# Scatters of the tokens' places that no longer name one another as a dependency

## The chip, the cores and the metric

The kernel runs on one core of a Trainium2 chip. The metric is device time in microseconds of one execution. Five instruction queues work side by side: TensorE (PE: matrix products and transposes), VectorE (DVE), ScalarE (ACT), GpSimd (POOL) and SyncE (SP, which issues DMAs). An engine takes its own instructions strictly in order; between engines, and between an engine and a DMA, order comes from semaphores alone.

## What is computed

Three layers follow one another; the numbers below are the reference's, cut to what matters.

```
attention:  4 x 8 heads, 576 positions, head_dim 64, causal by blocks of 64
            -> x of shape [2304 tokens, 512]
MLP:        h = x @ w_in (512 x 2048); g = max(h,0) + alpha*min(h,0); x = g @ w_out
experts:    logits = x @ w_gate (512 x 8); expert = argmax(logits); gate = softmax(logits)[expert]
            for e in 0..7:  out[tokens of e] = gate * (max(x @ w1[e], 0) @ w2[e])
```

Each token goes to exactly one expert, so before the expert stage the kernel must know, for each expert, which tokens it has and with which gate weight.

## The kernel before, in words

The 2304 tokens are worked in nine groups of 256 (`G`), two tiles of 128 tokens each (`GT` = 2). Attention of later batches, the first MLP and the routing of finished groups are interleaved in one plan: each piece of work is a task with the engines that may do it, an estimated duration, a priority and the buffers that it reads and writes. The planner (`Plan.order`) simulates the tasks and writes them out in the order of its simulated starts. The program is built with a manual schedule, so the order on each engine is that of this plan; the framework adds the semaphores that the data need.

For a group of the first MLP, TensorE makes 16 blocks `l` (line 697), VectorE applies the activation (`t`, lines 675 and 676), ScalarE or VectorE makes the high part `gh` (line 700), POOL or VectorE the low part `gl` (line 703), and TensorE adds `gh` and `gl` times `wo` into `acc` (line 727). In the attention, POOL or VectorE scales the probabilities `P` (line 530) before TensorE transposes them into `PT` (line 519).

The routing of a group (class `Route`) makes logits, the expert of each token, and the token's place in that expert's list. The list is a table in DRAM, `info`, of 8 x 2304 rows with two columns of four bytes: the token's number and its gate weight. `place` computes the places `si` and fills `ig`, both columns for both tiles: column 0 (the token's number) by one POOL add over both tiles (line 853), column 1 by VectorE (line 858). Then `scatter` (line 861) writes one tile's 128 rows of `ig` into `info` at the places `si`, by an indirect DMA of POOL; there are two scatters for each group, eighteen in all. `ig` and `si` have one buffer each.

At the start, the DMA of line 1343 fills the whole of `info` with a sentinel. The readers of `info` are loads on SP: `fetch_it` (line 1418) loads the first 256 rows of the expert that leads after eight groups, while the ninth group is still in the first MLP; `fetch` (line 1000, and 1002 for the remainder) loads the next 256 rows each time. With the loaded list `it`, POOL gathers rows of `x2` into `xg` (lines 1424 and 1004), and TensorE transposes them into `Tx` (line 1011).

For the group's gate logits the buffer `xr` is shared by two things: the tokens of the next group (line 646) and rows of the gate's weights (line 768), which VectorE multiplies with the tokens (line 813). `xr` has one buffer. From the tokens, ScalarE and VectorE make `xh` and `xl` (lines 654 and 657), the inputs of line 697.

Of the kernel before, what the change touches and what calls it, by code (L numbers as in the profile page):

```python
# [12 lines left out]
ALU = mybir.AluOpType  # L13
# [3 lines left out]
IOA = bass.IndirectOffsetOnAxis  # L17
ENGINES = [getattr(mybir.EngineType, e) for e in ("PE", "DVE", "Activation", "Pool", "SP")]

P = 128  # L20
# [7 lines left out]
G = P * GT  # L28
# [18 lines left out]
class Consts:  # L47
    def __init__(K, nc, cp):
        K.ident = cp.tile([P, P], F32, name="ident")
        make_identity(nc, K.ident)  # L50

        K.U = cp.tile([P, P], F32, name="U")
        nc.gpsimd.memset(K.U, 1.0)
        nc.gpsimd.affine_select(K.U, K.U, pattern=[[1, P]], compare_op=ALU.is_gt, fill=0.0, base=0, channel_multiplier=-1)

        K.II = cp.tile([P, 64], F32, name="II")
        nc.vector.tensor_add(K.II, K.ident[:, 0:64], K.ident[:, 64:128])
        K.ones = cp.tile([P, P], F32, name="ones")
        nc.gpsimd.memset(K.ones, 1.0)
        K.w8 = cp.tile([P, E], F32, name="w8")  # L60
        nc.gpsimd.iota(K.w8, pattern=[[-1, E]], base=E, channel_multiplier=0, allow_small_or_imprecise_dtypes=True)
        K.i8 = cp.tile([1, E], F32, name="i8")
        nc.gpsimd.iota(K.i8, pattern=[[1, E]], base=0, channel_multiplier=0, allow_small_or_imprecise_dtypes=True)
        K.base = cp.tile([1, E], F32, name="base")
        nc.gpsimd.iota(K.base, pattern=[[NT, E]], base=0, channel_multiplier=0, allow_small_or_imprecise_dtypes=True)

        K.run = [cp.tile([P, GT + 1, E], F32, name=f"run{i}") for i in range(2)]
        nc.gpsimd.iota(K.run[0][:, 0], pattern=[[NT, E]], base=0, channel_multiplier=0, allow_small_or_imprecise_dtypes=True)
        K.pid = cp.tile([P, GT], I32, name="pid")
        nc.gpsimd.iota(K.pid, pattern=[[P, GT]], base=0, channel_multiplier=1)  # L70
        K.zero = cp.tile([P, DM // P], F32, name="zero")
        nc.vector.memset(K.zero, 0.0)
        K.wg = cp.tile([P, 4, E], F32, name="wg")
        K.al = cp.tile([P, 16], F32, name="al")
# [154 lines left out]
class Weights1:  # L229
# [13 lines left out]
    def plan(A, pl):  # L243

        nc = A.nc
        for i, (key, src) in enumerate(A.srcs):
            s, pr, r = ("stw", i), WPRIO + WSTEP * i, A.raw[key]
            x, y = (r.rearrange("p (n t) -> p n t", t=2)[:, :, z] for z in range(2))
            pl.buf(s, "stw", (P, 512), I32)

            def load(on, r=r, src=src):
                nc.sync.dma_start(r, src.bitcast(I32))

            def scale(on, y=y):
                nc.scalar.mul(y.bitcast(F32), y.bitcast(F32), 2.0 ** -112)

            def sign(on, y=y, s=s):
                nc.gpsimd.tensor_tensor(pl[s].bitcast(F32), y.bitcast(F32), A.K.zero[:, 0:1].to_broadcast([P, 512]), op=ALU.mult)

            def bits(on, x=x, y=y, s=s, key=key):  # L260
                nc.vector.scalar_tensor_tensor(pl[s], x, 29, pl[s], op0=ALU.logical_shift_right, op1=ALU.bitwise_or)
                nc.vector.scalar_tensor_tensor(A.raw[key][:, 0:512], y, 3, pl[s], op0=ALU.logical_shift_left, op1=ALU.bitwise_or)

            pl.add(("SP", 450), load, [], [("r", key)], 100 * i, (524288, 360))
            pl.add(("ACT", 700), scale, [], [("r", key)], pr)
            pl.add(("POOL", 1100), sign, [("r", key)], [s], pr)
            pl.add(("DVE", 1450), bits, [("r", key)], [s, ("w", key)], pr)
# [343 lines left out]
class Mlp1:  # L611


    def __init__(A, tc, K, W1, bp, rt, psp, xT, wgT, x2, info):
        A.tc, A.nc, A.K, A.W1, A.W, A.bp, A.rt, A.psp, A.wgT = tc, tc.nc, K, W1, W1.W, bp, rt, psp, wgT
        A.xT, A.x2, A.info = xT, x2, info

    def plan(A, pl):
        for g in range(NG):
# [167 lines left out]
class Route:  # L787
# [5 lines left out]
    def small(A, nm, shape, dt=F32):  # L793
        return A.ml.rt.tile([P] + shape, dt, tag="r" + nm, bufs=1, name=nm + A.n)
# [45 lines left out]
    def place(A, rk):  # L840
        nc, K, g, GE, oh, ex, sm, small = A.nc, A.K, A.g, GT * E, A.oh, A.ex, A.sm, A.small
        run = K.run[g % 2]
        for i in range(GT):
            nc.vector.tensor_add(run[:, i + 1], run[:, i], rk[:, E * i:E * i + E])
        nc.vector.tensor_copy(K.run[(g + 1) % 2][:, 0], run[:, GT])
        pos, sl, A.si = small("pos", [GT, E]), small("sl", [GT]), small("si", [GT], I32)
        nc.vector.tensor_add(pos, run[:, 0:GT], rk[:, GE:2 * GE].rearrange("p (i e) -> p i e", e=E))
        nc.vector.tensor_mul(pos, pos, oh)
        nc.vector.reduce_sum(sl, pos, axis=AX.X)
        nc.vector.tensor_copy(A.si, sl)  # L850

        A.ig, gx, ge = small("ig", [GT, 2], I32), small("gx", [GT, E]), small("ge", [GT])
        nc.gpsimd.tensor_scalar(A.ig[:, :, 0], K.pid, g * G, None, op0=ALU.add)
        nc.vector.tensor_scalar_add(sm, sm, 1e-9)
        nc.vector.tensor_mul(gx, ex, oh)
        nc.vector.reciprocal(sm, sm)
        nc.vector.reduce_sum(ge, gx, axis=AX.X)
        nc.vector.tensor_mul(A.ig[:, :, 1].bitcast(F32), ge, sm)

    def scatter(A, i):  # L860
        A.nc.gpsimd.indirect_dma_start(out=A.ml.info, out_offset=IOA(ap=A.si[:, i:i + 1], axis=0), in_=A.ig[:, i, :], in_offset=None)

    def steps(A, psp, xts):

# [72 lines left out]
class Experts:  # L937
# [59 lines left out]
    def fetch(A, r, j, base, rows=NT + 1):  # L997
        it = A.itile(r, j)
        src = A.info[ds(base + 2 * P * j, 2 * P), :].rearrange("(h p) c -> p h c", p=P)
        A.nc.sync.dma_start(it, src)  # L1000
        if j:
            A.nc.sync.dma_start(A.rem, src)
        for h in range(2):
            A.nc.gpsimd.indirect_dma_start(out=A.xg[:, h], out_offset=None, in_=A.x2[0:rows, :], in_offset=IOA(ap=it[:, h, 0:1], axis=0))
# [296 lines left out]
def moe_kernel(tc, qk, v, qke, ve, w_in, w_out, alpha, w_gate, wgT, w1, w2, out):  # L1301
    nc = tc.nc
    with ExitStack() as ctx:
# [3 lines left out]
        info = dp.tile([E * NT, 2], I32, name="info")  # L1307
# [3 lines left out]
        K = Consts(nc, cp)  # L1311
# [4 lines left out]
        ap = st0.enter_context(tc.tile_pool(name="attn", bufs=1))  # L1316
        aps = st0.enter_context(tc.tile_pool(name="attnps", bufs=1, space=PSUM))
        pl, banks, hold = Plan(), Slots(), {}
# [10 lines left out]
        ml = Mlp1(tc, K, W1, bp, cp, None, xT, wgT, x2, info)  # L1329
        od = Order(nc, K, cp)  # L1330

        def setup():

            pl.buf(("sent",), "xt", (P, E * NT // P, 2), I32)
            pl.buf(("alr",), "t", (16, P))
            pl.buf(("alps",), "T")

            def sentinel(on):
                nc.gpsimd.memset(pl["sent",], 0)
                nc.gpsimd.memset(pl["sent",][:, :, 0:1], NT)  # L1340

            def empty(on):
                nc.sync.dma_start(info.rearrange("(p n) c -> p n c", p=P), pl["sent",])
                nc.sync.dma_start(x2[NT:NT + 1, :].rearrange("o (p n) -> p (o n)", p=P), K.zero)

            def load(on):
                nc.sync.dma_start(K.wg, w_gate.rearrange("(k p) e -> p k e", p=P))
                nc.sync.dma_start(pl["alr",], alpha.rearrange("(f p) -> f p", p=P))

            pl.add(("POOL", 600), sentinel, [], [("sent",)], 1000)  # L1350
            pl.add(("SP", 900), empty, [("sent",)], [("info0",)], 1000, (160000, 100))
            pl.add(("SP", 900), load, [], [("wg",), ("alr",)], -4000, (20000, 10))
            pl.add(("PE", 120), lambda on: nc.tensor.transpose(pl["alps",][:, 0:16], pl["alr",], K.ident[0:16, 0:16]), [("alr",)], [("alps",)], -250)
            pl.add(("DVE", 160), lambda on: nc.vector.tensor_copy(K.al, pl["alps",][:, 0:16]), [("alps",)], [("al",)], -250)

        def close(on):
            st0.close()
            psc = ctx.enter_context(tc.tile_pool(name="ps", bufs=1, space=PSUM))
            banks.add(psc, T=1, H=3)
            banks.add(psb, T=2, H=2)  # L1360
            ccp = ctx.enter_context(tc.tile_pool(name="experts", bufs=1))
            ex = hold["ex"] = Experts(tc, K, wp, ccp, banks, x2, info, w1, w2, out)
            ex.rawtiles(ccp, NR)

        def first_expert(done):
# [49 lines left out]

        def fetch_it():
            ex = hold["ex"]
            nc.sync.dma_start(ex.itile(0, 0), info[ds(hold["base"], 2 * P), :].rearrange("(h p) c -> p h c", p=P))

        def fetch_rows():  # L1420
            ex = hold["ex"]
# [11 lines left out]
        ex = hold["ex"]  # L1433
# [60 lines left out]
```

## Time and profile before

| | |
|---|---|
| median of 3 runs | 955.63 us |
| the three runs | 955.39, 955.63, 960.72 us |
| profiled execution, its own time | 954.17 us |
| its span, first to last instruction | 952.4 us |
| TensorE busy | 880.6 us (92%) |
| VectorE, ScalarE, POOL busy | 560.2, 402.2, 310.6 us |
| mean granted TensorE clock | 0.973 |

Starts in the profile are counted from the start of the span. A number in brackets at the end of a timeline row is the idle time of that engine just before the row, with what ended it by the profile; where a wait names several semaphores, the profile puts it down to the one that came last by its records, which need not be the right one. The granted clock is given in parts of 2.4 GHz: 1.00 is 2.4 GHz, 0.50 is 1.2 GHz.

### The profile page before, as it was taken

How to read it: one execution, taken by the hardware profiler on the slowest of the kernel's cores; microseconds unless marked ns; L12 is line 12 of the kernel's file. 1: busy time of each engine (PE TensorE's matmuls, PEld its weight loads, DVE VectorE, ACT ScalarE, POOL GpSimd, SP SyncE). 2: the span in 40 equal slices, each digit the busy share in tenths (PEclk: the TensorE clock that was granted, in tenths of full speed). 3: DMA queues.
4: the chain of work that ended last, by engine and by line, in shares of the span. 5: the costliest groups of instructions: out<-in, count | busy, mean ns of one | idle time of the engine just before them, and what ended most of it. 6: DMA issues, size and time to landing. Idle time of an engine off the chain costs nothing. (4 is left out here: it accounts for less than half of the span.)

```text
span 952.4 us, 17816 instructions
## 1 busy us (share of the span) xinstructions
PE 880.6 (92%) x6185; PEld 750.1 (79%) x6185; DVE 560.2 (59%) x1387; ACT 402.2 (42%) x1022; POOL 310.6 (33%) x323
## 2 busy tenths in 40 slices
PE   7999989999989999989999989899889998998883
PEld 6656658888878888878899889889779987988763
DVE  5999896667757767847756656446215211513450
ACT  7877764455435554445421111223215222523451
POOL 1455665333433354443332222232212111111110
PEclk9999999999999999999999989999999999999997
DMA  9981001313213214302112212033436211613551
GB/s 344 372 311 51 18 17 52 99 47 115 97 50 106 85 50 139 100 22 73 58 49 70 48 64 67 24 113 109 142 115 219 71 47 56 211 48 92 157 182 42
DMA packets 49724, 98.39 MB, mean 103 GB/s; under 512 B 12575, under 2 KB 19375, under 8 KB 49584
## 3 DMA queue, kind: packets, MB, share of 16 engines
q1 hardware_dynamic: 38720, 76.78, 24.6%
q0 software_dynamic: 4240, 11.56, 3.9%
q10 hardware_dynamic: 6624, 8.39, 2.5%
q8 instruction: 63, 1.03, 0.5%
q14 instruction: 77, 0.63, 0.2%
HBM read 83.43 MB, written 13.67 MB: 102 GB/s over the span
## 5 line engine op out<-in xcount | busy, mean ns | idle before, releaser
L697 PE MATMUL l<-xh,wi 128*128 128x256 f32 x1024 | 208.6, 288 | 1.7 <-DVE t L676 1.7
L697 PEld LDWEIGHTS l<-xh,wi 128*128 128x128 f32 x1024 | 169.5, 193 | 6.6 <-DVE t L676 2.2
L727 PE MATMUL acc<-wo,gh 128*128 128x512 f32 x512 | 168.4, 410 | 0.0
L697 PE MATMUL l<-xl,wi 128*128 128x256 f32 x512 | 146.0, 285 | 0.0
L703 POOL TENSOR_TENSOR gl<-t,gh 128x256 fp32r<-128x256 f32 x107 | 81.5, 762 | 183.3 <-ACT gh L700 150.7
L700 ACT CAST gh<-t 128x256 fp32r<-128x256 f32 x120 | 48.8, 406 | 178.4 <-DVE t L676 105.8
L675 DVE TENSOR_SCALAR t<-l,al 128x256 f32<-128x256 f32 x128 | 61.8, 483 | 104.2 <-PE l L697 98.3
L530 POOL TENSOR_SCALAR P<-P,sm 128x256 f32<-128x256 f32 (+4 forms) x71 | 89.0, 1260 | 101.9 <-ACT gh L700 46.2
L727 PE MATMUL acc<-wo,gl 128*128 128x512 f32 x256 | 102.1, 399 | 8.9 <-POOL gl L703 8.9
L697 PEld LDWEIGHTS l<-xl,wi 128*128 128x128 f32 x512 | 99.1, 194 | 3.9 <-issue 0.2
L727 PEld LDWEIGHTS acc<-wo,gh 128*128 128x128 f32 x512 | 88.0, 193 | 10.9 <-issue 0.5
L524 ACT COPY F<-PT 128x384 f32<-128x384 f32 (+2 forms) x126 | 58.5, 479 | 70.5 <-PE PT L519 68.6
L479 DVE TENSOR_REDUCE nb<-S 128x1 f32<-128x256 f32 (+4 forms) x160 | 69.5, 476 | 28.4 <-PE S L456 14.8
L813 DVE SCALAR_TENSOR_TENSOR xt<-y,xr_wg 128x512 f32<-128x512 f32 x96 | 73.7, 768 | 8.9 <-DMA xr_wg<-in_wgT_dram 5.1
L519 PE MATMUL PT<-ident,P 128*128 128x128 f32 (+1 forms) x400 | 65.7, 284 | 12.2 <-POOL P L530 6.7
L496 ACT ACTIVATE P<-S,nb 128x128 f32<-128x128 f32 (+3 forms) x128 | 66.7, 529 | 9.3 <-DVE nb L479 8.4
L519 PEld LDWEIGHTS PT<-ident,P 128*128 128x128 f32 (+1 forms) x400 | 45.9, 142 | 26.5 <-POOL P L530 9.4
L727 PEld LDWEIGHTS acc<-wo,gl 128*128 128x128 f32 x256 | 48.9, 191 | 21.2 <-POOL gl L703 10.2
L1038 PE MATMUL l<-cxh,e 128*128 128x256 f32 x320 | 58.2, 282 | 0.8 <-ACTq L1273 0.8
L1038 PE MATMUL Y<-e,hh 128*128 128x512 f32 x176 | 57.2, 406 | 0.0
L676 DVE SCALAR_TENSOR_TENSOR t<-l,t 128x256 f32<-128x256 f32 x128 | 54.3, 425 | 4.4
L995 DVE TENSOR_TENSOR e<-raw,e 128x512 fp32r<-128x512 f32 x68 | 43.9, 685 | 19.6 <-ACT e L994 19.4
(375 smaller groups left out, 1686.5 us busy)
## 6 DMA issues: line engine op xcount, KB each, us to landing
raw<-in_moe_w_dram SPq DMA_DIRECT2D x96, 256.0 KB
xr_wg<-in_wgT_dram SPq DMA_DIRECT2D x24, 512.0 KB
qk<-in_qk_dram SPq DMA_DIRECT2D x16, 608.0 KB
rawi<-in_moe_w_in_dram SPq DMA_DIRECT2D x16, 512.0 KB
rawo<-in_moe_w_out_dram SPq DMA_DIRECT2D x16, 512.0 KB
v<-in_v_dram SPq DMA_DIRECT2D x16, 320.0 KB
x<-y ACTq DMA_DIRECT2D x16, 256.0 KB
xr<-xT SPq DMA_DIRECT2D x7, 512.0 KB
```

Of the source, the lines that this page charges most:

```text
L479: nc.vector.tensor_reduce(pl["nb", p, c][:, 2 * k + j:2 * k + j + 1], pl[Ss[j]][:, a:b], axis=AX.X, op=ALU.max, negate=True)
L496: nc.scalar.activation(pl[x][:, a:b], pl[Ss[j]][:, a:b], AF.Exp, bias=nb, scale=1.0, accum_out=pl["sm", p, c][:, 2 * k + j:2 * k + j + 1])
L519: nc.tensor.transpose(pl[t][0:w, k], pl[x][:, P * k:P * k + w], A.K.ident)
L524: f(pl[F][:, 0:n], pl[t][:, 0:n])
L530: (nc.gpsimd if on == "POOL" else nc.vector).tensor_scalar(y, y, pl["sm", p, c][:, k:k + 1], None, op0=ALU.mult)
L675: nc.vector.tensor_scalar(pl[out], x, 0.0, A.K.al[:, f:f + 1], op0=ALU.min, op1=ALU.mult)
L676: nc.vector.scalar_tensor_tensor(pl[out], x, 0.0, pl[out], op0=ALU.max, op1=ALU.add)
L697: nc.tensor.matmul(pl[l][:, 0:G], lhsT=a[:, c], rhs=b, start=k == 0 and j == 0, stop=k == 3 and j == 2)
L703: (nc.gpsimd if on == "POOL" else nc.vector).tensor_sub(pl[gl], pl[t], pl[gh].bitcast(F32))
L727: nc.tensor.matmul(pl[acc], lhsT=x[:, c], rhs=w, start=f == 0 and j == 0, stop=f == 15 and j == 2)
L813: A.nc.vector.scalar_tensor_tensor(t, A.y(i), 1.0, wg, op0=ALU.mult, op1=ALU.mult, accum_out=A.L()[:, i, e:e + 1])
L1038: A.nc.tensor.matmul(ps, lhsT=x[a], rhs=w[b], start=first and q == 0, stop=last and q == 2)
```

## The change

The tokens' numbers (column 0 of `ig`) are now made for one tile at a time, by a new method `token`, just ahead of that tile's scatter. A scatter is put into a group of instructions, `places`, whose members have no dependency on one another through `info`. What they would have had through it is named by hand: each scatter follows the sentinel's fill (`filled`); the first load of the list (`fetch_it`) follows all scatters made until then, and the load of the first expert's second tile follows the scatters made since.

```diff
@@ class Mlp1
+        A.sent, A.filled = [], None
+
+    def follow(A, x, ys):
+        for y in ys:
+            A.tc.add_manual_dep(x.ins, y.ins.name, mybir.DependencyInfo(mybir.DependencyClass.Sync, mybir.DependencyReason.DATA), reason="places")
+
+    def placed(A, x):
+
+        A.follow(x, A.sent)
+        A.sent = []
@@ Route.place
-        nc.gpsimd.tensor_scalar(A.ig[:, :, 0], K.pid, g * G, None, op0=ALU.add)
@@ Route
+    def token(A, i):
+        A.nc.gpsimd.tensor_scalar(A.ig[:, i, 0:1], A.K.pid[:, i:i + 1], A.g * G, None, op0=ALU.add)
+
     def scatter(A, i):
-        A.nc.gpsimd.indirect_dma_start(out=A.ml.info, out_offset=IOA(ap=A.si[:, i:i + 1], axis=0), in_=A.ig[:, i, :], in_offset=None)
+
+
+        A.token(i)
+        ml = A.ml
+        x = A.nc.gpsimd.indirect_dma_start(out=ml.info, out_offset=IOA(ap=A.si[:, i:i + 1], axis=0), in_=A.ig[:, i, :], in_offset=None)
+        ml.tc.declare_no_dep(x.ins, group="places", reason="rows of their own")
+        ml.tc.add_to_no_dep_group("places", x.ins)
+        ml.follow(x, [ml.filled])
+        ml.sent.append(x)
@@ Experts.fetch
-        A.nc.sync.dma_start(it, src)
+        x = A.nc.sync.dma_start(it, src)
+        if (r, j) == (0, 1):
+            A.ml.placed(x)
@@ moe_kernel
-                nc.sync.dma_start(info.rearrange("(p n) c -> p n c", p=P), pl["sent",])
+                ml.filled = nc.sync.dma_start(info.rearrange("(p n) c -> p n c", p=P), pl["sent",])
...
+            ex.ml = ml
...
-            nc.sync.dma_start(ex.itile(0, 0), info[ds(hold["base"], 2 * P), :].rearrange("(h p) c -> p h c", p=P))
+            ml.placed(nc.sync.dma_start(ex.itile(0, 0), info[ds(hold["base"], 2 * P), :].rearrange("(h p) c -> p h c", p=P)))
```

The instructions of TensorE, VectorE and ScalarE stand in the same order as before. Only POOL's order changes, at the nine pairs of scatters, and the waits of two loads on SP. POOL's queue around the sixth pair, before the change (`gl` is the low part, `ig` the two columns, `info` the list; names after `waits` are semaphores, DMASW those of POOL's DMAs, with a number for each lane):

```order
L703 TENSOR_TENSOR gl_13_6755<-t_13_6725,gh_13_6749 128x256 [waits PE_49,Activation_49]
L853 TENSOR_SCALAR ig_6792<-pid 128x2 [waits DMASW1_49]
L703 TENSOR_TENSOR gl_14_6808<-t_14_6771,gh_14_6780 128x256 [waits PE_49,Activation_49]
L861 DMA info<-ig_6792,si_6787 18432x2 [waits DVE_49,Pool_49]
L861 DMA info<-ig_6792,si_6787 18432x2 [waits DMASW2_49]
L703 TENSOR_TENSOR gl_15_6846<-t_15_6819,gh_15_6833 128x256 [waits DVE_49,PE_49]
```

The same place in the changed program:

```order
L713 TENSOR_TENSOR gl_13_6760<-t_13_6730,gh_13_6754 128x256 [waits PE_49,Activation_49]
L713 TENSOR_TENSOR gl_14_6812<-t_14_6776,gh_14_6785 128x256 [waits PE_49,Activation_49]
L870 TENSOR_SCALAR ig_6797<-pid 128x1 [waits DMASW1_49,DMASW0_49]
L877 DMA info<-ig_6797,si_6792 18432x2 [waits DVE_49,Pool_49]
L870 TENSOR_SCALAR ig_6797<-pid 128x1
L877 DMA info<-ig_6797,si_6792 18432x2 [waits Pool_49]
L713 TENSOR_TENSOR gl_15_6852<-t_15_6823,gh_15_6838 128x256 [waits DVE_49,PE_49]
```

The second scatter waited for the first one's DMA (DMASW2) and now waits for the add ahead of it, on POOL's own semaphore. The add has become two, behind the last `gl` ahead of the scatters and between them.

On SP, around the first load of the list, before:

```order
L984 ISA
L984 DMA raw_6141<-in_moe_w_dram 128x512 [waits DMAHW3_49,PE_49,Pool_49]
L1418 ISA
L1418 DMA it_6121<-info 128x2x2 [waits DMAHW4_49,DMASW7_49]
L984 ISA
L984 DMA raw_6142<-in_moe_w_dram 128x512
```

And in the changed program:

```order
L1004 ISA
L1004 DMA raw_6145<-in_moe_w_dram 128x512 [waits DMAHW3_49,PE_49,Pool_49]
L1441 ISA
L1441 DMA it_6125<-info 128x2x2 [waits DMASW5_49,DMASW4_49,DMASW6_49,DMASW3_49,DMASW7_49,DMASW2_49,DMAHW4_49,DMASW1_49,DMASW0_49]
L1004 ISA
L1004 DMA raw_6146<-in_moe_w_dram 128x512
```

The load stands at the same place and names more semaphores; the weight loads (`raw`) stand behind it as before.

## Rows read from the trace of the kernel before

**Rows 1.** The page, busy time of the engines over the span.

```profile
PE 880.6 (92%) x6185; PEld 750.1 (79%) x6185; DVE 560.2 (59%) x1387; ACT 402.2 (42%) x1022; POOL 310.6 (33%) x323
```

**Rows 2.** TensorE's timeline: start, us, engine, line, operation, count, idle before.

```profile
276.22 0.48 PE L519 MATMUL PT<-ident,P 128*128 128x128 f32 x2 [2.46 <-POOL P L530]
...
351.81 0.66 PE L519 MATMUL PT<-ident,P 128*128 128x128 f32 x4 [0.86 <-POOL P L530]
...
413.22 1.12 PE L519 MATMUL PT<-ident,P 128*128 128x128 f32 x4 [3.18 <-POOL P L530]
...
550.32 0.80 PE L727 MATMUL acc<-wo,gl 128*128 128x512 f32 x1 [4.06 <-POOL gl L703]
...
602.12 0.50 PE L727 MATMUL acc<-wo,gl 128*128 128x512 f32 x1 [2.61 <-POOL gl L703]
...
623.23 0.50 PE L727 MATMUL acc<-wo,gl 128*128 128x512 f32 x1 [2.19 <-POOL gl L703]
...
680.28 0.63 PE L1011 MATMUL Tx<-ident,xg 128*128 128x128 f32 x4 [2.50 <-DMA xg<-x,it]
```

**Rows 3.** Windows of TensorE: from:to, length, busy (count), granted clock, DMA share, GB/s.

```profile
276.20:279.70 3.50, 3.48 (x11) 0.54 0.00 0
413.20:417.00 3.80, 3.78 (x17) 0.58 0.01 2
420.00:500.00 80.00, 80.00 (x621) 1.00 0.19 60
550.30:557.00 6.70, 6.68 (x29) 0.55 0.23 82
602.00:604.00 2.00, 1.89 (x12) 1.00 0.00 0
624.00:629.00 5.00, 5.00 (x22) 0.66 0.20 48
```

**Rows 4.** POOL's timeline: second scatters of pairs 2, 3, 4, 6 to 9.

```profile
274.21 0.96 POOL L861 DMA_INDIRECT info<-ig,si  x1 [2.90 <-DMA info<-ig,si]
...
348.48 0.96 POOL L861 DMA_INDIRECT info<-ig,si  x1 [2.52 <-DMA info<-ig,si]
...
409.33 0.96 POOL L861 DMA_INDIRECT info<-ig,si  x1 [2.91 <-PE PT L519]
410.33 2.83 POOL L530 TENSOR_SCALAR P<-P,sm 128x512 f32<-128x512 f32 x1
...
548.54 0.96 POOL L861 DMA_INDIRECT info<-ig,si  x1 [4.09 <-DMA info<-ig,si]
...
600.35 0.96 POOL L861 DMA_INDIRECT info<-ig,si  x1 [3.32 <-DMA info<-ig,si]
...
621.46 0.96 POOL L861 DMA_INDIRECT info<-ig,si  x1 [3.25 <-DMA info<-ig,si]
...
669.57 1.15 POOL L861 DMA_INDIRECT info<-ig,si  x1 [2.93 <-DMA info<-ig,si]
```

**Rows 5.** POOL's groups by form, 160 to 680 us: busy us, mean ns | idle before.

```profile
L530 POOL TENSOR_SCALAR P<-P,sm 128x512 f32<-128x512 f32 x12 | 23.8, 1981 | 26.3 <-ACT gh L700 17.2 <-PE o L563 7.2 <-DVE sm L504 1.9
...
L853 POOL TENSOR_SCALAR ig<-pid 128x2 int32<-128x2 int32 x9 | 2.0, 220 | 0.4
```

**Rows 6.** Timeline around the first scatter of pair 6, VectorE and POOL.

```profile
542.48 0.16 DVE L858 TENSOR_TENSOR ig<-ge,sm 128x2 f32<-128x2 f32 x1
...
543.41 1.04 POOL L861 DMA_INDIRECT info<-ig,si  x1 [2.04 <-DVE ig L858]
```

**Rows 7.** POOL's timeline: the second of two gathers that wait for nothing between them.

```profile
630.91 0.96 POOL L1424 DMA_INDIRECT xg<-x,it  x1 [0.30 <-issue]
```

**Rows 8.** VectorE's timeline behind pair 4.

```profile
410.32 0.81 DVE L407 SCALAR_TENSOR_TENSOR qkl<-qk,qkh 128x640 fp32r<-128x640 f32 x1
```

**Rows 9.** Timeline of SP and ScalarE: load and cast of the last group's tokens.

```profile
588.99 0.38 SPq L646 DMA_DIRECT2D xr<-xT  x1
...
594.50 1.48 ACT L654 CAST xh<-xr 128x256 fp32r<-128x256 f32 x4 [1.36 <-PE l L697]
```

## The prediction

> **What bounds the kernel now.** I read the page first: TensorE is busy for 92% of the span, far ahead of every other engine [rows 1], so a microsecond is worth something here only if TensorE gets it back. The next view is TensorE's own timeline, reduced to the rows with idle time before them. Between 160 and 681 us nearly all of that idle time stands in seven rows [rows 2]: six in the attention and first-MLP stage (2.46, 0.86, 3.18, 4.06, 2.61 and 2.19 us, 15.4 us together) and one of 2.50 us at the start of the expert stage. In the stretch between the third and the fourth of them TensorE is busy for 80.00 of 80 us [rows 3], so in that stage nothing but these gaps keeps it from running through.
>
> Each of the six is put down to POOL, to `gl` (line 703) or to `P` (line 530). The POOL timeline shows what POOL did just before: it was idle between the two scatters of a pair, 2.52 to 4.09 us, until the first one had landed [rows 4]. The names in the brackets vary; where TensorE is named, its work had nothing to do with a scatter, and the wait in the program is for the first scatter's DMA. The second scatter is followed at once by the `P` or `gl` that TensorE wants: at 409.33 the scatter, at 410.33 the `P`, at 413.22 TensorE. There are nine pairs, one for each group of tokens. I count them 1 to 9 in order of time; pairs 1 and 5 have no TensorE row, POOL's delay was hidden there. Pair 9 delays the load of the list (line 1000), then the gather, then the transposes at 680.28.
>
> There is a second cost. After the stalls of pairs 2, 4, 6 and 8 TensorE ran at the lower of its two levels, 1.2 GHz: the granted clock was 0.54, 0.58, 0.55 and 0.66 in the stretches behind them, while it stayed 1.00 behind pair 7 [rows 3]. A stretch loses its length times what is missing to 1: 3.5 x 0.46 + 3.8 x 0.42 + 6.7 x 0.45 + 5.0 x 0.34 = 1.61 + 1.60 + 3.02 + 1.70 = 7.9 us.
>
> **The change, part by part.** *Removed:* the second scatter's wait for the first one's landing; POOL's idle time in rows 4 goes. *Added:* the one add over both columns (0.22 us [rows 5]) becomes two, each just ahead of its scatter. The first falls into POOL's wait for VectorE's last input (2.04 us idle at pair 6 [rows 6]) and costs nothing; if that cover were gone it would cost its 0.22 us. The second stands between the scatters, and the scatter waits for it on POOL's own semaphore. What replaces the removed idle time is therefore R = the add + the scatter's start after its last input. The add has 0.22 [rows 5]. For the start there are two rows: with nothing to wait for, the second of two gathers starts 0.30 us after the first [rows 7]; after VectorE's last input (542.48 + 0.16) the scatter of pair 6 starts at 543.41, 0.77 us later [rows 6]. The new wait is a semaphore wait like the second, so I take 0.77: R = 1.0 us. Ends: 0.52 (0.22 + 0.30), and 1.8 if a VectorE instruction of 0.81 us [rows 8] is served first.
>
> *Moved:* the waits of the list's readers. The load of `it` on SP (line 1418) now names all eight semaphores of the software queue; those of pairs 1 to 7 were reached long before, and on the last scatter of pair 8 it waits already. What is queued behind it on SP, the weight loads, moves with it, and it moves forward. Cost nothing. TensorE, VectorE and ScalarE keep their instructions in their order.
>
> What TensorE gets back is at each pair the smaller of its stall and POOL's lead, idle time minus R [rows 2, 4]:
> - pair 2: 2.90 - 1.0 = 1.90 of 2.46
> - pair 3: lead 1.52, stall 0.86: 0.86
> - pair 4: lead 1.91, and the `P` behind it took 2.83 us where the twelve of its shape took 1.98 on average [rows 4, 5]; it ran beside VectorE's lines 407 and 408, which start at 410.32 [rows 8]. With the lead it is done when they start. 1.91 + 0.85 = 2.76 of 3.18
> - pair 6: 4.09 - 1.0 = 3.09 of 4.06
> - pair 7: 2.32 of 2.61
> - pair 8: lead 2.25, stall 2.19: 2.19
>
> Together 13.1 us. The stalls left are under 1 us, and the stall of 0.86 us in rows 2 belongs to none of the four slow stretches, so I take the whole 7.9 us of the clock as regained. Pair 9: both scatters land 1.93 us earlier, and so do list, gather and transposes: 1.93 of 2.50 [rows 2, 4]. Pairs 1 and 5: nothing, POOL's delay was hidden.
>
> Sum: 13.1 + 7.9 + 1.9 = 23 us (22.9) off the profiled execution's 954.17 us: 931.2. The median of the three runs is 955.63, 1.46 above it; against that median the forecast is **932.7 us**.
>
> What is late next: the leftover of pair 6, about 1 us, and in the expert stage the same waits as now, which all hang on TensorE's progress and move with it.
>
> One rule of the Trainium skill speaks against the lead. The row first: a `P` of POOL went from 1.98 to 2.83 us beside VectorE instructions of two inputs [rows 4, 5, 8]. The Trainium skill (SBUF — State Buffer, section "SBUF: two separate sides") says VectorE and GpSimd share one pair of ports as an exclusive lock, held for a whole instruction, and that GpSimd cannot write the descriptors of its DMAs while it is locked out. By that rule a second scatter that comes earlier can be held for a VectorE instruction of that kind; that is rival B, and the sum there is 13 us and not 23.
>
> **The rivals.**
> - A, the forecast, R between 0.52 and about 1.2. At R = 0.52 the gains are 2.38 + 0.86 + 3.18 + 3.57 + 2.61 + 2.19 = 14.8, with 7.9 and 2.4: 25.1 us, 930.5. Chance 0.68.
> - B, the scatter is held by VectorE, R = 1.8 at every pair. Gains 1.10 + 0.72 + 1.11 + 2.29 + 1.52 + 1.45 = 8.2, pair 9 gives 1.1; stalls of 1 to 2 us remain, so I leave half of the clock term: 4.0. 13.3 us, 942.3. For it: the 2.83 us row. Against: it must happen at every pair, and few VectorE instructions there are that long. Chance 0.12.
> - C, another chain takes over. `xr` has one buffer: its load waits for the last product of the gate, and the cast that starts the next group (594.50) comes 5.51 us after that load's issue (588.99) [rows 9], with TensorE nearly at the same place. If this chain does not move when TensorE gets ahead, the gain of pair 6 is lost again: 3.09 + 3.02 = 6.1 us, 938.8. Against: the products stand in VectorE's order among instructions that wait for TensorE, so they move forward with it. Chance 0.08.
> - D, the wait stays under another name. In the program the second scatter waits for POOL alone, so this needs a dependency that the program does not show: 955.6, no change. Together with a gain that other engines eat: 0.08.
> - E, slower. The place is the second scatter itself: if its descriptors cannot be written before the first scatter is through, the idle time only moves into its own row, and the add and the start (R = 1.0) come on top at six pairs and pair 9: 7 us. Longer stalls at pairs 3 and 7 would then lose the clock as well, 1.6 us each: 10.2 us, 965.8. It decides from a second scatter of 4 us on, instead of 0.96 [rows 4]. Against: a second gather 0.30 us behind the first took 0.96 us [rows 7]. Chance 0.03.
>
> Their sum is 0.99; the rest lies below 927.
>
> **How the numbers follow.** The time is that of A, 932.7. Above, the range takes in B and C, up to 943. Below, it takes A's better end, 930.5, and 3 us for one drop of the clock that a shifted stall in the expert stage may save (the dearest of the four cost 3.0): 927. Left out are D and E and a little at the bottom, about 0.12. A's own range is 927 to 936. One per cent, about what a measurement of this kernel can tell from no change, is 9.6 us: faster means under 946.1. A, B and C lie there, with the rest below: 0.89. Within 1%: D, 0.08. Slower: E, 0.03.
>
> **What would show it.** In the profile after, the second scatter starts about 2.0 us after the first at all nine pairs and lasts about 1 us; POOL's waits for the scatter's DMA (line 861 now) are gone; of TensorE's six stalls those of pairs 3 and 8 are gone and none is over 1.2 us; the granted clock is 1.00 behind all of them; the transposes of pair 9 wait about 0.6 us. A second scatter that starts 3 us after the first means B, one that lasts 4 us means E, a new TensorE wait for `xh` or `xl` means C. The prediction is wrong if the stalls go and the time does not follow: then something other than TensorE paced these stages.

## The result

The changed kernel takes 929.59 us (median of 4 runs, 926.22 to 932.10); the kernel before, beside it on the same chip, took 955.51 us (4 runs, 952.58 to 960.72). The ratio is 0.9721, with an interval of 0.9666 to 0.9775. The forecast was 932.7 us, range 927 to 943. The profiled execution took 926.22 us, its span 924.5 us. So the sign and the size of the whole were right, and so was the mechanism at the first eight pairs. The gain of the ninth came later than forecast and by another way; that the total fits there too is in part luck.

### The profile page after: what moved, and what is told of

It is laid out like the page before. It is cut to its first block, busy times and chain, and to the rows that moved or that the text cites. A ratio compares the mean times of both kernels' runs of the same rounds, so it can differ in the third digit from the quotient of the medians.

```text
span 924.5 us, 17837 instructions
## 1 busy us (share of the span) xinstructions
PE 869.6 (94%) x6185; PEld 740.4 (80%) x6185; DVE 560.1 (61%) x1387; ACT 401.7 (43%) x1022; POOL 314.3 (34%) x332
## 5 line engine op out<-in xcount | busy, mean ns | idle before, releaser
L707 PE MATMUL l<-xh,wi 128*128 128x256 f32 x1024 | 205.4, 285 | 1.4 <-DVE t L686 1.4
L707 PEld LDWEIGHTS l<-xh,wi 128*128 128x128 f32 x1024 | 166.7, 190 | 6.1 <-DVE t L686 1.8
L737 PE MATMUL acc<-wo,gh 128*128 128x512 f32 x512 | 166.0, 405 | 0.0
L1015 DVE TENSOR_TENSOR e<-raw,e 128x512 fp32r<-128x512 f32 x68 | 43.9, 685 | 19.5 <-ACT e L1014 19.3
```

The source lines that it names most:

```text
L707: nc.tensor.matmul(pl[l][:, 0:G], lhsT=a[:, c], rhs=b, start=k == 0 and j == 0, stop=k == 3 and j == 2)
L737: nc.tensor.matmul(pl[acc], lhsT=x[:, c], rhs=w, start=f == 0 and j == 0, stop=f == 15 and j == 2)
```

## The profile after

**The page.** TensorE's share rose, and its busy time fell from 880.6 us [rows 1] to 869.6 us although it runs the same 6185 instructions: less of that work ran at the lower clock (the windows below).

```profile
PE 869.6 (94%) x6185; PEld 740.4 (80%) x6185; DVE 560.1 (61%) x1387; ACT 401.7 (43%) x1022; POOL 314.3 (34%) x332
```

**POOL's timeline, pairs 4 and 6** (the answer to [rows 4, 6]; line 877 is the scatter now, line 870 the split add):

```profile
402.89 1.08 POOL L877 DMA_INDIRECT info<-ig,si  x1 [2.18 <-DVE t L685]
404.00 0.23 POOL L870 TENSOR_SCALAR ig<-pid 128x1 int32<-128x1 int32 x1
404.52 1.06 POOL L877 DMA_INDIRECT info<-ig,si  x1 [0.28 <-DVE nb L479]
405.62 1.59 POOL L530 TENSOR_SCALAR P<-P,sm 128x512 f32<-128x512 f32 x1
...
536.07 1.07 POOL L877 DMA_INDIRECT info<-ig,si  x1 [1.74 <-DVE ig L867]
537.22 0.43 POOL L870 TENSOR_SCALAR ig<-pid 128x1 int32<-128x1 int32 x1
537.93 1.24 POOL L877 DMA_INDIRECT info<-ig,si  x1 [0.28 <-DVE xl L667]
539.20 0.73 POOL L713 TENSOR_TENSOR gl<-t,gh 128x256 fp32r<-128x256 f32 x1
```

Read each piece from one end to the next start. After the first scatter's end at 403.97 comes the add, then 0.28 us, then the second scatter at 404.52: 0.55 us where 2.91 us stood [rows 4]. Over all nine pairs that piece is 0.54 to 0.60 us at six of them and 0.79 to 0.82 at three. No wait of POOL names the scatter's DMA any more. The `P` behind pair 4, which took 2.83 us [rows 4], takes 1.59.

**TensorE's timeline**, rows with 0.2 us or more of idle time before them, from 160 us to the first product of the expert stage:

```profile
276.27 0.44 PE L519 MATMUL PT<-ident,P 128*128 128x128 f32 x2 [0.22 <-POOL P L530]
...
337.77 0.55 PE L519 MATMUL PT<-ident,P 128*128 128x128 f32 x3 [0.21 <-POOL P L530]
...
539.99 0.50 PE L737 MATMUL acc<-wo,gl 128*128 128x512 f32 x1 [1.04 <-POOL gl L713]
...
586.66 0.50 PE L737 MATMUL acc<-wo,gl 128*128 128x512 f32 x1 [0.20 <-POOL gl L713]
...
659.01 0.63 PE L1033 MATMUL Tx<-ident,xg 128*128 128x128 f32 x4 [0.67 <-DMA xg<-x,it]
...
663.29 0.63 PE L1033 MATMUL Tx<-ident,xg 128*128 128x128 f32 x4 [2.25 <-DMA xg<-x,it]
...
666.14 0.39 PE L1060 MATMUL l<-cxh,e 128*128 128x256 f32 x1 [0.82 <-ACTq L1295]
```

Of the six stalls [rows 2] 1.46 us is left (0.22 + 1.04 + 0.20), where 15.4 us stood. The transposes of pair 9 are another matter: one wait of 2.50 us [rows 2] has become two, 0.67 and 2.25 us.

**The granted clock** in the stretches that answer to [rows 3] (windows of TensorE: from:to, length, busy, granted clock, DMA share, GB/s) is full behind every pair, including the four that ran at 0.54 to 0.66:

```profile
276.20:279.70 3.50, 3.43 (x23) 1.00 0.02 2
405.60:409.40 3.80, 3.80 (x29) 1.00 0.05 5
540.00:546.70 6.70, 6.70 (x47) 1.00 0.48 148
586.60:590.10 3.50, 3.44 (x23) 1.00 0.32 117
604.00:609.00 5.00, 5.00 (x34) 1.00 0.53 21
662.00:668.00 6.00, 3.89 (x25) 1.00 1.02 376
```

**Step by step.** The best ruler is POOL's own timeline: the time from the start of a pair's first scatter to that of the next pair's. Pair 6, for one, started at 543.41 [rows 6] and pair 7 at 595.99, 52.58 us; now 536.07 and 582.96, 46.89 us. The last two columns run from pair 9's first scatter to the first expert product, and from there to the end of the span.

| us | 1-2 | 2-3 | 3-4 | 4-5 | 5-6 | 6-7 | 7-8 | 8-9 | 9-expert | expert-end |
|---|---|---|---|---|---|---|---|---|---|---|
| before | 97.47 | 74.65 | 60.47 | 82.00 | 56.04 | 52.58 | 21.18 | 48.42 | 19.38 | 267.43 |
| change | 97.47 | 70.95 | 59.40 | 77.14 | 56.04 | 46.89 | 18.77 | 44.42 | 19.99 | 258.36 |
| difference | 0 | -3.70 | -1.07 | -4.86 | 0 | -5.69 | -2.41 | -4.00 | +0.61 | -9.07 |
| predicted | 0 | -3.5 | -0.9 | -4.4 | 0 | -6.1 | -2.3 | -3.9 | -1.9 | 0 |

From pair 1 to pair 9 it is 21.73 us against 21.0 predicted. (Ahead of pair 1 the change's execution is 2.29 us later, 175.07 for 172.78; over all executions that start lies between 172.78 and 178.93, whatever the kernel.) The two steps behind are where the prediction failed.

The first expert product is a poor mark for pair 9, because TensorE's next wait behind it changed as well: that for the gather of the third tile, whose list is loaded only after a burst of weight loads (told with the experiments). TensorE before, then after, each with the transposes that come next:

```profile
703.22 1.08 PE L1011 MATMUL Tx<-ident,xg 128*128 128x128 f32 x4 [3.91 <-DMA xg<-x,it]
...
728.12 0.60 PE L1011 MATMUL Tx<-ident,xg 128*128 128x128 f32 x4
```

```profile
681.53 0.63 PE L1033 MATMUL Tx<-ident,xg 128*128 128x128 f32 x4 [1.06 <-DMA xg<-x,it]
...
705.03 0.60 PE L1033 MATMUL Tx<-ident,xg 128*128 128x128 f32 x4
```

Counted from pair 9's first scatter, the later of these transposes start at 62.53 us before and at 58.88 in the change. In all seven executions in which pair 9 has its wait, or fills in its place, it is 61.60 to 63.47 us (mean 62.4), in the three of the change 58.32 to 60.05 (mean 59.1). From there to the end it is 220.4 to 225.0 us (mean 222.6) and 219.5 to 224.4 (mean 222.0). So the change is worth some 3.3 us behind pair 9, and the rest of the 9.07 belongs to that one execution.

## The experiments

Theory: POOL works in order, so the wait at the second scatter kept it from the `P` or `gl` that TensorE wanted, and the longer stalls cost the clock as well; each pair is worth its own stall and clock. Rivals: the split add or the named waits did it; the landing of the scatters itself counts; the pairs hang together. A second question came from the trace: where pair 9's gain went, and what the 9 us of the expert stage are.

**The change again, twice**, as the mark for the others; the second time it stood beside the run with the early list, told of last.

> The change itself once more, as the mark for the other runs on the same chip. About 930 us, ratio 0.972 to the kernel before, with the second scatter 1.6 to 2.0 us behind the first at all nine pairs and the TensorE stalls behind the pairs at 1.5 us together. If a good part of the expert stage's extra 8 us belongs to one execution and not to the kernel, the granted clock there will show other drops in this execution than in the first one.

> The change itself, beside the run with the earlier list on the same chip. About 931 us. Its steps from pair to pair are to be the same as in its other executions within 0.1 us, and the expert stage to differ by several us from execution to execution, with the drops of the clock.

Measured: 931.40 us (ratio 0.9735, 0.9663 to 0.9807) and 929.60 us (0.9737, 0.9686 to 0.9789). The steps between pairs repeat to 0.03 us. The step behind pair 9 is 20.52 and 19.27 us, the expert stage 263.91 and 261.30 us: its 9 us less in the first execution were for the greater part that execution's. One cause stands in the first repeat, behind the transposes of pair 9, whose waits there were 0.58 and 2.25 us, nearly those of the execution above, which kept 1.00:

```profile
275.30:278.80 3.50, 3.42 (x23) 1.00 0.01 2
539.10:545.80 6.70, 6.69 (x46) 1.00 0.45 148
660.00:670.00 10.00, 6.92 (x30) 0.67 1.00 370
```

**The declaration left out**, the rest of the change kept:

```diff
-        ml.tc.declare_no_dep(x.ins, group="places", reason="rows of their own")
-        ml.tc.add_to_no_dep_group("places", x.ins)
```

> The two adds stay split and moved, and the list's readers still wait by name; only the declaration that scatters needn't wait for one another is left out, so the second scatter waits for the first one's landing again. Theory (the wait is what cost): POOL idle 2.5 to 4.1 us between the scatters of a pair, the six stalls back at about 15 us, time 955 us, ratio 1.00. Rival (the moved add, or the readers' waits, did it): the time stays near 930 us, ratio 0.97, though the wait is back.

Measured: 957.49 us, ratio 1.0020 (0.9977 to 1.0063). POOL's wait, TensorE's stall and the lower clock are back together. POOL, then TensorE's timeline, then TensorE's windows:

```profile
545.00 0.43 POOL L870 TENSOR_SCALAR ig<-pid 128x1 int32<-128x1 int32 x1
548.26 1.06 POOL L877 DMA_INDIRECT info<-ig,si  x1 [2.84 <-DMA info<-ig,si]
549.35 0.73 POOL L713 TENSOR_TENSOR gl<-t,gh 128x256 fp32r<-128x256 f32 x1
```

```profile
550.14 0.79 PE L737 MATMUL acc<-wo,gl 128*128 128x512 f32 x1 [3.42 <-POOL gl L713]
```

```profile
277.40:280.90 3.50, 3.49 (x12) 0.56 0.00 0
415.10:418.90 3.80, 3.77 (x37) 1.00 0.01 2
550.10:556.80 6.70, 6.66 (x37) 0.75 0.29 105
601.50:606.50 5.00, 5.00 (x23) 0.68 0.28 105
```

The whole gain is the declaration's. The rival of the moved add, and of the waits named by hand, falls.

**Fills in place of the wait**, 24 and then 16 of them:

```diff
+        K.fill = cp.tile([P, 8], I32, name="fill")
...
+        for _ in range(24 if i else 0):
+            A.nc.gpsimd.memset(A.K.fill, 0)
         x = A.nc.gpsimd.indirect_dma_start(...)
```

> The change, with 24 fills of a 128x8 tile on POOL between the two scatters of each pair, about 2.5 to 3 us, so that POOL is kept from its next work about as long as the wait kept it, without any wait for a DMA. Theory (what cost is that POOL, which works in order, came late to the product that TensorE wants): the six stalls come back within about 0.7 us each, with the clock drops behind them, time 950 to 957 us. Rival (it was the landing of the scatters, or DMA traffic, and POOL's place only accompanied it): no stalls, time 930 us. Should the fills take a different time, the stalls move by the difference.

Measured: 966.58 us, ratio 1.0101 (1.0027 to 1.0175), above the range expected. The fills took 0.16 us each from start to start, so the second scatter began 5.3 to 5.9 us behind the first, against 3.6 to 5.1 in the kernel before: I had built the wait too long. The stalls behind the pairs came to 24.0 us together, with one even at pairs 1 and 5 (1.18 and 0.52 us). So the second run had 16:

> The change, with 16 fills on POOL between the scatters instead of 24. One fill took 0.16 us, so the second scatter starts about 4.2 us behind the first, the mean of the six pairs of the kernel before (4.21). Theory (only the time that POOL is kept counts): stalls of 2.7, 1.5, 3.4, 3.2, 2.5 and 2.1 us at pairs 2, 3, 4, 6, 7 and 8, 15 us together as before, and 953 to 958 us, between the 931 us of the change and the 967 us of 24 fills. Rival (part of the loss in the run of 24 fills came from what the fills themselves do to VectorE): slower than 960 us.

Measured: 955.05 us, ratio 0.9999 (0.9967 to 1.0032). The six stalls are 2.60, 1.41 (in two rows), 3.22, 3.31, 2.45 and 2.15 us, 15.1 together, where 15.4 was expected from the list. POOL, and TensorE at pair 6:

```profile
547.95 1.56 POOL L879 MEMSET fill<- 128x8 int32 x10
549.65 1.06 POOL L880 DMA_INDIRECT info<-ig,si  x1
550.75 0.73 POOL L714 TENSOR_TENSOR gl<-t,gh 128x256 fp32r<-128x256 f32 x1
```

```profile
551.53 0.66 PE L738 MATMUL acc<-wo,gl 128*128 128x512 f32 x1 [3.31 <-POOL gl L714]
```

No wait for a DMA is left in this kernel's pairs, and its time is that of the kernel before. What counts is how long POOL is kept, not by what.

**One pair, or two, at a time.** The declaration was made for some groups alone; `g` is the pair's number less one.

```diff
+        if A.g in (5,):
             ml.tc.declare_no_dep(x.ins, group=f"places{A.g}", reason="rows of their own")
             ml.tc.add_to_no_dep_group(f"places{A.g}", x.ins)
```

> The kernel with the split add, where only the scatters of pair 6 need not wait for one another; the other eight pairs wait as before. Theory (each pair is worth its own stall and the clock behind it): from the first scatter of pair 6 to that of pair 7 it takes 46.9 us instead of 52.6, the TensorE stall there is 1.0 us instead of 4.1 and the granted clock behind it 1.00 instead of 0.55; the steps of the other pairs stay as in the kernel before within 1 us or by what a drop of the clock moves; time about 950 us. Rival (the pairs help one another, or another chain takes over when TensorE gets ahead at one pair alone): the step shrinks by less than 3 us or the next one grows.

> Only the scatters of pairs 3 and 7 need not wait, the two stalls behind which the granted clock stayed at 1.00. Theory: the step behind pair 3 shrinks by about 1.1 us and that behind pair 7 by 2.4 us, the size of their stalls and nothing more; time 952 us. Rival (the clock's loss hangs on the sum of all idle time before, not on a single long stall): the clock behind pairs 4 and 8 changes too, and more than 3.5 us is gained.

> Only the scatters of pairs 1 and 5 need not wait, the two pairs with no TensorE stall behind them. POOL gets back 2.3 and 1.9 us there as at the others. Theory (POOL's delay was hidden there): both steps stay at 97.5 and 56.0 us, time as before, 956 us. Rival (POOL's earlier work shortens later waits too): 952 us or less.

Measured: 954.54 us (ratio 1.0004, 0.9967 to 1.0040), 952.29 us (0.9984, 0.9949 to 1.0018) and 958.65 us (1.0040, 1.0003 to 1.0076). The whole time settles none of them: the kernel with the split add and all waits is at 957.49 itself, and several us come and go in other places. The steps settle them. Pair 6 alone: 46.90 us behind it, the value of the full change to 0.01 us, where executions with the wait had 50.79 to 53.64. Pairs 3 and 7 alone: 59.40 and 18.80 us, again the full change's. Pairs 1 and 5 alone: 97.46 and 56.04 us, as with the wait. The expected stall of pair 6 is there to 0.04 us (pair 6's kernel):

```profile
549.22 0.50 PE L737 MATMUL acc<-wo,gl 128*128 128x512 f32 x1 [1.04 <-POOL gl L713]
...
599.32 0.50 PE L737 MATMUL acc<-wo,gl 128*128 128x512 f32 x1 [3.61 <-POOL gl L713]
```

Each pair tried is worth its own step and lends nothing to the next; pairs 2, 4 and 8 were not tried alone. Only the total that I expected for pair 6, 950 us, was a miss, and the kernel before was the wrong mark for it. In all four executions with the split add and the wait at pair 7 that step was 23.23 to 23.70 us instead of 21.18: the second scatter started 4.97 to 5.24 us behind the first (4.36 before), TensorE stalled for 3.34 to 3.61 us instead of 2.61 [rows 2], and the granted clock behind it was 0.66 to 0.70 instead of 1.00. Against them pair 7 is worth 4.4 to 4.9 us. Why the first scatter lands later there is open.

**Pair 9 alone**, by the same edit with `g` 8.

> Only the scatters of pair 9, the last, need not wait for one another. Theory (the gain of pair 9 is lost to the gathers, which land late beside the burst of raw weight loads): the second scatter starts 1.7 us behind the first and the list's load goes out about 2.3 us earlier, but the first expert product comes as late as before, 19.4 to 21 us behind the first scatter of pair 9 (19.4 in the kernel before, 20.0 and 20.5 in the two executions of the change). Rival (it was lost only because TensorE was elsewhere in the change): 17 us, the 1.9 to 2.3 us forecast. The whole time cannot tell the two apart: 953 to 957 us.

Measured: 955.92 us (ratio 1.0014, 0.9968 to 1.0059), and the step to the first expert product is 21.41 us, none of the 1.9 gained there (19.12 to 21.42 us in the executions with the wait at pair 9). The transposes behind the third tile come 60.20 us behind the first scatter, nearly as in the change. TensorE:

```profile
686.70 0.63 PE L1034 MATMUL Tx<-ident,xg 128*128 128x128 f32 x4 [0.55 <-DMA xg<-x,it]
...
691.05 1.09 PE L1034 MATMUL Tx<-ident,xg 128*128 128x128 f32 x4 [2.33 <-DMA xg<-x,it]
```

The same two waits as in the full change, so it is pair 9's own doing. What changed is the neighbour of the gathers. In the kernel before, POOL's gather and SP's burst of sixteen raw weight loads were 3.16 us apart (POOL's and SP's timelines):

```profile
676.69 0.98 POOL L1004 DMA_INDIRECT xg<-x,it  x1 [5.97 <-DMA it<-info]
...
679.85 11.20 SPq L984 DMA_DIRECT2D raw<-in_moe_w_dram  x16
```

In the change they are 1.55 us apart:

```profile
655.56 0.99 POOL L1026 DMA_INDIRECT xg<-x,it  x1 [6.64 <-PE Y L1060]
656.86 0.96 POOL L1026 DMA_INDIRECT xg<-x,it  x1 [0.30 <-issue]
...
657.11 11.53 SPq L1004 DMA_DIRECT2D raw<-in_moe_w_dram  x16
```

Counted from pair 9's first scatter, the gather goes out 1.7 us earlier (11.10 to 9.41 us) but the burst 3.3 us earlier (14.26 to 10.96). Between 662 and 668 us the DMA engines are busy at a share of 1.02 (the last of the windows above), and the second gather lands late. Over all executions the wait goes with that distance: 1.52 to 1.70 us in four (three of the change and this one), with 1.49 to 2.33 us of wait at the second transposes; 2.27 to 3.16 us in eight others, with none. What the earlier burst takes from the second gather it gives back at the third: the list behind it is loaded 28.6 to 29.7 us after pair 9's first scatter in these four, 31.1 to 32.2 in the seven with the wait or fills.

**The burst held back** until the second gather has landed:

```diff
+        x = A.nc.sync.dma_start(t, src.rearrange("o p n -> p (o n)"))
+        if (r, i) == (1, 0):
+            A.ml.follow(x, [A.gathered])
...
```

> The change, with one more wait: the first of the sixteen raw weight loads that SP issues behind the list's load at the start of the expert stage follows the landing of the second gather. Theory (pair 9's gain was lost because the gathers landed late beside that burst of loads, which started 1.55 us behind the first gather's issue instead of 3.2 us): the gathers land in 3.2 to 4 us instead of 4.2 to 6.6, TensorE's two waits at the transposes (0.67 and 2.25 us) shrink to under 1 us together, and the first expert product comes about 2 us earlier; time 928 us if nothing later takes it back. Rival 1 (the gathers are late by their own descriptors, not by the burst): the two waits stay, 930 us. Rival 2: the raw weights come 4 us later and the expert weights are late, TensorE waits for them, 932 to 934 us.

Measured: 934.95 us, ratio 0.9796 (0.9714 to 0.9878), no faster than the change. The theory on pair 9 held: neither transpose waits any more, the longest landing of a gather there fell from 6.3 and 5.5 us (in the two repeats of the change) to 3.6, and the step to the first expert product is 16.70 us instead of 19.3 to 20.5. But the gain turned into a new wait. SP, POOL and TensorE of this kernel, one after the other:

```profile
660.23 11.28 SPq L1004 DMA_DIRECT2D raw<-in_moe_w_dram  x16
677.18 0.39 SPq L1022 DMA_DIRECT2D it<-info  x1
```

```profile
679.79 0.98 POOL L1028 DMA_INDIRECT xg<-x,it  x1 [14.89 <-DMA it<-info]
```

```profile
683.34 1.09 PE L1037 MATMUL Tx<-ident,xg 128*128 128x128 f32 x4 [5.16 <-DMA xg<-x,it]
```

The list of the third tile is loaded behind a branch, at whose join the program makes SP wait for every load that it has under way. (The profile puts SP's wait down to the output's scatter, `out_dram`; the join is read from the program and from the next runs. The burst's last load was issued at 671.2 us and these loads took up to 6.6 us to land.) The later the burst, the later that list, and TensorE, which had got ahead, waits 5.16 us for its gather.

**The third tile's list loaded early**, ahead of the burst, with the hold and without it (its load behind the branch is left out):

```diff
+        if (r, j) != (0, 2):
+            x = A.nc.sync.dma_start(it, src)
...
+        if (r, j) == (0, 1):
+            A.nc.sync.dma_start(A.itile(0, 2), A.info[ds(base + 4 * P, 2 * P), :].rearrange("(h p) c -> p h c", p=P))
```

> The change, the first raw weight load held until the second gather has landed as in the run with that wait, and the list of the third tile of the first expert loaded early, ahead of the raw loads, instead of behind the join of a branch, at which SP waits for all sixteen raw loads to land. Theory (with the wait alone the 3.3 us won at the transposes were given back at the next gather, whose list could only be loaded after the raw loads had landed): the first expert product comes 16.7 us behind the first scatter of pair 9, the gather of the third tile goes out at 671 to 676 us instead of 679.8, its stall of 5.2 us falls under 2 us, and the time is 2 to 4 us under that of the change, 926 to 929 us. Rival (the third gather waits for something else too, the landing of the output's scatter or POOL's own part of that join): the stall stays at 3 us or more, and the time at 930 us.

> The change with the list of the third tile loaded early, ahead of the raw weight loads, but without holding those loads for the gather: one half of the fastest version. Theory (two separate costs): the gathers of the second tile still land beside the burst, TensorE waits 0.6 to 0.7 and 1.5 to 2.3 us at the transposes and the first expert product comes 19.3 to 20.5 us behind the first scatter of pair 9; the third tile's gather goes out before 676 us and its stall of 1.1 to 1.2 us is gone; time 929 us, some 1 us under the change, which the whole time cannot tell. Rival (the early list alone does it, since it puts another load between the gather and the burst): the first expert product comes at 17.6 us as in the run with both.

Measured: 925.98 us with the hold (ratio 0.9709, 0.9654 to 0.9763), 924.10 us without it (0.9655, 0.9581 to 0.9730), the two fastest kernels here. The third gather goes out at 665.05 and 666.87 us, and its stall is gone in both. The intervals overlap a little with those of the change, so by the whole time the step from it is likely and not shown; the transposes behind the third tile come 55.08 and 55.60 us behind pair 9's first scatter, for 58.32 at best in the change. With the hold the step to the first expert product is 17.59 us, not the 16.70 expected: the first transposes wait 0.71 us again, and only the second wait stays away. So the hold accounts for the second wait alone. That the first was gone too in the run before goes with a gather 8.43 us behind the first scatter, where this run has 9.53 and the change 9.36 to 9.45; why is open. My theory of two separate costs was wrong for the second kernel: without the hold, too, the step behind pair 9 is 18.11 us and only one wait is left. SP and TensorE of the kernel without the hold:

```profile
653.57 1.53 SPq L1027 DMA_DIRECT2D it<-info  x1
659.69 13.82 SPq L1004 DMA_DIRECT2D raw<-in_moe_w_dram  x16
```

```profile
660.09 0.63 PE L1036 MATMUL Tx<-ident,xg 128*128 128x128 f32 x4 [1.23 <-DMA xg<-x,it]
```

The burst starts 3.05 us behind the first gather (656.64) of its own accord. In the program the read of a register on SP stands ahead of the burst and waits for all loads before it, the added list among them; that it is this wait which moves the burst was not tried by itself.

## Why the prediction was right, and where not

- **What bounds it.** Right, and shown. The six stalls go with the wait, come back with it, and come back with fills that wait for nothing; the hidden pairs 1 and 5 are worth 0.
- **R, the replacement.** The step was right, its size off: 0.54 to 0.82 us instead of 1.0. I took the start after a VectorE result, 0.77 us [rows 6], because the new wait is a semaphore wait too. The scatter starts 0.28 us after POOL's own add, like the gather that waits for nothing [rows 7].
- **The gain per pair.** Right: 21.73 us from pair 1 to pair 9 for 21.0. Better by 0.2 to 0.5 us at pairs 2, 3 and 4, the last by a `P` of 1.59 us, shorter than the 1.98 that I took. At pair 6 I was 0.4 us too high; the stall left there is 1.04 us, as forecast (about 1).
- **The clock.** Right. What a step gained beyond its stall is 3.70 - 2.24, 4.86 - 3.18, 5.69 - 3.02 and 4.00 - 2.19: 1.46, 1.68, 2.67 and 1.81 us at pairs 2, 4, 6 and 8, 7.6 us for 7.9.
- **Pair 9: wrong at the place where I looked for it.** The step that failed is "both scatters land 1.93 us earlier, and so do list, gather and transposes". It held for the first gather: counted from pair 9's first scatter its transposes came 1.83 us earlier (14.69 to 12.86), and their wait fell to 0.67 us, as forecast (about 0.6). It failed for the second gather, whose landing did not follow: its transposes came 0.58 us later (16.56 to 17.14), behind a wait of 2.25 us. Up to the first expert product the term is +0.61, +1.14 and -0.11 us in three executions, not -1.9. I also wrote of the loads behind the list on SP that they move forward and cost nothing. That is where it went: the burst came nearer to the gathers than it had been.
- **The expert stage: not counted.** I let its waits move with TensorE. One of them shrank: at the third tile TensorE waited 2.31 to 3.91 us in the six executions with the wait at pair 9 or with 16 fills, and 1.06, under 0.2 and 1.22 in those of the change (1.24 with 24 fills, where TensorE came to the first expert product 22.50 us behind pair 9's first scatter). That brings pair 9's gain after all, some 3.3 us in place of the 1.9, through the earlier burst and the earlier list behind it. With the 21.7 of the pairs it makes 25.0, against a gain in the medians of 25.3 to 25.9 us and 22.9 forecast. That a term with its path wrong came out on the right side, by another wait, is luck.
- **The rivals.** B: VectorE's instructions of two inputs did lie beside the second scatter, at pair 6 from 537.16 to 538.57, and the add took 0.43 us instead of 0.23, the scatter 1.24 instead of 1.06. That is 0.4 us and not 0.8, and the piece between the scatters was longer at three pairs only. The Trainium skill (SBUF — State Buffer, section "SBUF: two separate sides") lets one engine hold the shared ports for a whole instruction (its words there on descriptors are about VectorE's 2-port modes). The trace agrees that POOL is slowed beside such an instruction, and its price here is at most 0.4 us. C: the cast of the last group comes 5.50 us after its load (575.96 to 581.46), as it did [rows 9]; the chain moved with TensorE. D falls with the profile after, where the second scatter starts 0.28 us behind the add, E with scatters of 1.06 to 1.24 us.

## What to carry to other kernels

A wait on an engine that works in order is priced by what stands behind it on that engine and by who needs that first: find the pieces where the bottleneck waits for the very next instruction, and take the smaller of its stall and the wait. Add the clock where a stall is followed by a stretch at the lower level. When a small transfer is issued earlier, look at what large transfers move with it: its issue time is yours to choose, its landing is not.

## What the runs showed of the hardware

- A POOL instruction started 0.28 us after another POOL instruction's result, and 0.77 us after VectorE's [rows 6].
- With the wait gone this part became repeatable: the steps from pair 1 to pair 9 sum to 471.05 to 471.12 us in six executions of the change and its three later versions. With the wait at pair 6 its step lay anywhere from 50.79 to 53.64 us in five executions (the kernel before and four with the split add), and the second scatter 4.41 to 6.27 us behind the first. The DMA's landing varied; the step does not follow it alone (52.43 us with 6.27).
- With 1.52 to 1.70 us between the first gather of 128 rows and a burst of sixteen weight loads, the slowest gather took 5.5 and 6.3 us to land (the two repeats of the change); with the burst held back, 3.6 us.
- The length of a stall does not settle the clock: behind 3.34 us at pair 4 the granted clock stayed 1.00 and behind 2.88 us at pair 2 it was 0.56, in the same execution (the windows of the kernel without the declaration).
